# Attention over a cached K and V on one core: K loaded by transposing DMAs instead of transposed on TensorE

## The chip, the cores and the metric

The kernel runs on one core of a Trainium2 chip, in one launch. The metric is the time on the device in microseconds; smaller is better. The engines are TensorE (PE in the profile, PEld for its weight loads), VectorE (DVE), ScalarE (ACT), GpSimd (POOL) and SyncE (SP), which here only issues loads.

## The reference

Two independent attention blocks, A and B, of the same shapes are computed and their outputs put side by side. All inputs are bfloat16.

```python
B, Sq, D = 16, 64, 640
H, Sk, Dh = 32, 512, 128
q = (x @ wq).reshape(B, Sq, H, Dh).transpose(0, 2, 1, 3)
scores = einsum("bhqd,bhkd->bhqk", q, k_cache) * (Dh ** -0.5)
p = softmax(scores, axis=-1)
o = einsum("bhqk,bhkd->bhqd", p, v_cache)
out = o.transpose(0, 2, 1, 3).reshape(B, Sq, H * Dh) @ wo        # per block
result = concatenate([out_A, out_B], axis=-1)
```

For each batch entry and head there is a K and a V of 512 x 128 (128 KB each), used once, by 64 queries. K and V of both blocks together are 268 MB of the 295 MB that are read.

## The kernel before, in words

The unit of work is a step pair, called m, of two heads. One head is treated for two batch entries at a time (j = 0 and 1), so that the 64 queries of each fill the 128 partitions together. A group is one pair of batch entries with 16 of the 32 heads, eight m. A pass is one block and one half of the heads; there are 4 passes with 8 groups each, 256 m in all. The output of the first half of the heads is kept in `outp` and added to that of the second half (OVF), and the result is stored.

The operations for one m are:

- LDK and LDV (SyncE): loads of K and V for four heads and one batch entry, 512 KB each; a chunk, two m, has two of each. There are rings of 5 chunks for K and V.
- KX (TensorE, line 433): eight transposes of 128 x 128 for one batch entry into a PSUM bank, twice for each m; KE (VectorE, line 442): the copy of that bank into `ktp_ring`. After this d is on the partitions and the keys are along the row.
- QP2 (line 451): the queries, ten matmuls; QE2 (ScalarE, 459) evicts them.
- SM2 (467): the scores of two heads, four matmuls with 512 columns each; MX (VectorE, 476): the negative row maximum; EX (ScalarE, 482): the exponential with the row sum; RC2 (VectorE, 488): the reciprocal of the sums of two heads.
- NM (GpSimd, 496): the probabilities times the reciprocal. The write puts the keys in the order in which V has them on the partitions.
- TR2 (505): eight transposes of the probabilities; TE2 (VectorE, 512) evicts them; PV2 (524): sixteen matmuls with V; OE2 (ScalarE, 532); OP2 (540 and 545): the output projection, accumulated in PSUM over the 16 heads of a group.
- XT and XE (604, 612): the transposes of x for a later group, once in eight m; they use the same PSUM bank as TR2.

The order on each engine is written out by hand as templates, (kind, offset in m, sub):

```python
PE_T = (("TR2", 1), ("QP2", 4), ("KX", 4, 0), ("SM2", 3), ("PV2", 1), ("XT", 0), ("OP2", 0), ("KX", 4, 1))
DVE_T = (("TE2", 1), ("RC2", 2), ("KE", 4, 0), ("MX", 3, 0), ("MX", 3, 1), ("KE", 4, 1), ("OVF", 0))
```

In turn k, TensorE transposes the probabilities of m = k+1, projects the queries of k+4, makes the scores of k+3, and so on. `build_plan` expands the templates, puts the loads in an order by the times at which they are due and their slots come free, and finds from the tiles read and written which operation waits for which. Each PSUM tile (the transposes, the scores of each head, the queries, the output of attention) has one buffer. The program for each engine is then a plain list; SyncE's loads are all on one queue.

K is loaded with 8 keys on end in a partition's run of 2 KB, two heads on 128 partitions; V with 4 keys, 1 KB.

Of the kernel before, what the change touches and what calls it, by code (L numbers as in the profile page):

```python
# [5 lines left out]
BF16 = mybir.dt.bfloat16  # L6
# [8 lines left out]
class Cfg:  # L15
    G = 4
    HH = 16
    NKB = 5
    NVB = 5
    NX = 2  # L20
    NXN = 1
    XLEAD = 10
    NQ = 2
    NKT = 2
    NP = 4
    NPN = 3
    NT = 2
    NO = 2
    NR = 8
    PE_T = (("TR2", 1), ("QP2", 4), ("KX", 4, 0), ("SM2", 3), ("PV2", 1), ("XT", 0), ("OP2", 0), ("KX", 4, 1))  # L30
    ACT_T = (("QE2", 4), ("OE2", 1), ("XE", 0), ("EX", 3, 0), ("EX", 3, 1), ("OV", 0), ("ST", -1))
    DVE_T = (("TE2", 1), ("RC2", 2), ("KE", 4, 0), ("MX", 3, 0), ("MX", 3, 1), ("KE", 4, 1), ("OVF", 0))
    POOL_T = (("NM", 0, 0), ("NM", 0, 1))
    TAIL_SPLIT = 2
    SLOT_NS = 3600.0
# [3 lines left out]
class Op:  # L39
# [3 lines left out]
    def __init__(self, eng, kind, idx, reads=(), writes=(), dur=0.0, ts=None, aux=None):  # L43
# [12 lines left out]
        self.dma = kind in ("LDK", "LDV", "LDX", "LDWQ", "LDWO", "ST")  # L56


STAGES = ("LDW", "LDX", "LDK", "LDV", "KX0", "KE0", "KX1", "KE1", "QP2", "QE2", "SM2", "MX0", "MX1", "EX0", "EX1",
          "RC2", "NM0", "NM1", "TR2", "TE2", "XT", "XE", "PV2", "OE2", "OP2", "OV", "ST")  # L60
STAGE_IDX = {s: i for i, s in enumerate(STAGES)}
SUB_KINDS = ("KX", "KE", "EX", "NM", "MX")


def build_plan(dims, cfg):
    NBLK, B, H = dims["NBLK"], dims["B"], dims["H"]
    G = cfg.G
# [23 lines left out]
    def mk(eng, kind, idx, reads, writes, stage, m_ts, sub=0, aux=None, dur=0.0):  # L91
        return Op(eng, kind, idx, reads, writes, dur=dur, aux=aux, ts=(m_ts, STAGE_IDX[stage], sub))

    OFF = {}
    for t in cfg.PE_T:
        OFF.setdefault(t[0], t[1])

    def make_op(kind, m, sub):
        g0, g1 = 2 * m, 2 * m + 1
        ps_, bp, grp, h0 = step_info(g0)  # L100
        c = g0 // G
        if kind == "KX":
            return mk("pe", "KX", (m, sub), [("kn", c % cfg.NKB, g0 % G), ("kn", c % cfg.NKB, g1 % G), ("ident",)],
                      [("KTB",)], "KX%d" % sub, m, sub)
        if kind == "KE":
            return mk("dve", "KE", (m, sub), [], [("KTB",), ("ktp", m % cfg.NKT, sub)], "KE%d" % sub, m, sub)
        if kind in ("MX", "EX", "NM"):
            g = 2 * m + sub
            r = g % cfg.NR
# [18 lines left out]
        if kind == "QE2":  # L128
            return mk("act", "QE2", m, [], [("QB",), ("qT", m % cfg.NQ)], "QE2", m)
        if kind == "SM2":  # L130
            return mk("pe", "SM2", m, [("qT", m % cfg.NQ), ("ktp", m % cfg.NKT, 0), ("ktp", m % cfg.NKT, 1)],
                      [("SB", 0), ("SB", 1)], "SM2", m)
        if kind == "RC2":
            return mk("dve", "RC2", m, [("rowsum", r0), ("rowsum", r1)], [("recip", r0), ("recip", r1)], "RC2", m)
# [29 lines left out]

    templates = {"pe": cfg.PE_T, "dve": cfg.DVE_T, "pool": cfg.POOL_T, "act": cfg.ACT_T}
    for eng, tmpl in templates.items():
        offs = [t[1] for t in tmpl] + [cfg.XLEAD]
        for k in range(-max(offs), NMAC - min(offs)):
            for t in tmpl:
                kind, off = t[0], t[1]  # L170
                sub = t[2] if len(t) > 2 else 0
                if kind in ("XT", "XE"):
                    op = make_op(kind, k, 0)
# [3 lines left out]
                m = k + off  # L177
                if 0 <= m < NMAC:
                    op = make_op(kind, m, sub)
# [26 lines left out]
    for grp in range(NGRP):  # L206
        m0 = MPG * grp
        op = mk("sp", "LDX", grp, [], [("xn", grp % cfg.NXN)], "LDX", m0 - cfg.XLEAD + OFF["TR2"], aux=grp,
                dur=cfg.DMA_NS["LDX"])
# [10 lines left out]

    for c in range(NCHUNK):
        m0 = MPC * c
        for kind, ring, n_ring, cons, tb in (("LDK", "kn", cfg.NKB, "KX", 2), ("LDV", "v", cfg.NVB, "PV2", 2.5)):
            ready = NEG if c < n_ring else MPC * (c - n_ring + 1) - 1 - OFF[cons]
            for pi, (piece, j, hlo, hhi) in enumerate(chunk_pieces(c)):
                op = mk("sp", kind, (c, j, piece), [], [(ring, c % n_ring, gi) for gi in range(hlo, hhi)], kind,
                        m0, aux=(c, j, hlo, hhi, piece), dur=cfg.DMA_NS[kind] * (hhi - hlo) / 8.0)
                loads.append((ready, m0 - OFF[cons] + 0.01 * hlo, tb + 0.001 * pi, op))
    pending = sorted(loads, key=lambda e: (e[1], e[2]))
    t_now = min(e[1] for e in loads) - 4.0  # L230
    while pending:
        cand = [e for e in pending if e[0] <= t_now]
        if cand:
            e = cand[0]
        else:
            e = min(pending, key=lambda e_: (e_[0], e_[1], e_[2]))
# [110 lines left out]
def mha_kernel(nc, blocks, out, cfg=None):  # L347
    cfg = cfg or Cfg()
# [3 lines left out]
    _, H, SK, DH = k0.shape  # L352
    assert SQ == 64 and DH == 128 and SK == 512 and D % 128 == 0 and B % 2 == 0
    KT = D // 128
    G = cfg.G
    scale = float(DH) ** -0.5
    DN = D
    assert DN <= 1024
    N0 = min(DN, 512)
    N1 = DN - N0  # L360

# [1 line left out]
    prune_waits(progs)  # L363
    NBP, SPB, NHALF = info["NBP"], info["SPB"], info["NHALF"]
    HH = SPB
    NKB, NVB, NX, NXN, NQ, NKT, NP, NPN, NT, NO, NR = (cfg.NKB, cfg.NVB, cfg.NX, cfg.NXN, cfg.NQ, cfg.NKT, cfg.NP,
                                                       cfg.NPN, cfg.NT, cfg.NO, cfg.NR)

    def step_info(g):
        grp = g // SPB  # L370
# [7 lines left out]
    with contextlib.ExitStack() as es:  # L378
        block = es.enter_context(nc.Block())

        def sb(name, shape, dt):
            return es.enter_context(nc.sbuf_tensor(name, shape, dt))

        wq_sb = sb("wq_sb", [128, 2, KT, HH * DH], BF16)
        wo_sb = sb("wo_sb", [128, 2, HH, DN], BF16)
        outp = sb("outp", [128, NBP, DN], F32) if NHALF > 1 else None
        xT_ring = sb("xT_ring", [128, NX, KT, 128], BF16)
        xn_ring = sb("xn_ring", [128, NXN, D], BF16)
        kn_ring = sb("kn_ring", [128, NKB, 2, G // 2, 8, DH], BF16)
        v_ring = sb("v_ring", [128, NVB, 2, G, 4, DH], BF16)  # L390
        ktp_ring = sb("ktp_ring", [128, NKT, 2, 2, SK], BF16)
        qT_ring = sb("qT_ring", [128, NQ, 2, 128], BF16)
        p_ring = sb("p_ring", [128, NP, SK], BF16)
        pn_ring = sb("pn_ring", [128, NPN, SK], BF16)
# [7 lines left out]
        ident = sb("ident", [128, 128], BF16)  # L402
        ps = es.enter_context(nc.psum_tensor("ps", [128, 8, 512], F32))
# [9 lines left out]
        else:  # L413
            out_ps_all = ps[:, 0, 0:DN]
        S_BANK0 = 2
        PT_BANK, O_BANK, Q_BANK, KT_BANK = 4, 5, 6, 7
        pt_ps_flat = ps[:, PT_BANK, :].bitcast(BF16)
        pt_ps = pt_ps_flat.rearrange("p (s t q) -> p s t q", s=2, t=4)
        o_ps = ps[:, O_BANK, 0:256]
        q_ps = ps[:, Q_BANK, 0:256]  # L420
        kt_ps_flat = ps[:, KT_BANK, :].bitcast(BF16)
        kt_ps = kt_ps_flat.rearrange("p (t s) -> p t s", t=8)

        def s_bank(sub):
            return ps[:, S_BANK0 + sub, :]

        def em_KX(e, op):
            m, j = op.idx
            g0 = 2 * m
            c, hp = g0 // G, (g0 % G) // 2  # L430
            first = last = None
            for t8 in range(8):
                ins = e.transpose(kt_ps[:, t8, :], kn_ring[:, c % NKB, j, hp, t8, :], ident[:, :])  # L433
                first = first or ins
                last = ins
            return first, last

        def em_KE(e, op):
            m, j = op.idx
            src = kt_ps_flat.rearrange("p (t hs pp) -> p t hs pp", t=8, hs=2)  # L440
            dst = ktp_ring[:, m % NKT, :, j, :].rearrange("p hs (t pp) -> p t hs pp", t=8)
            ins = e.tensor_copy(dst, src)  # L442
            return ins, ins

        def em_QP2(e, op):
            m = op.idx
# [15 lines left out]
        def em_SM2(e, op):  # L462
            m = op.idx
            first = last = None
            for sub in range(2):
                for j in range(2):
                    ins = e.matmul(s_bank(sub)[64 * j:64 * j + 64, :], qT_ring[:, m % NQ, sub, 64 * j:64 * j + 64],  # L467
                                   ktp_ring[:, m % NKT, sub, j, :], start=True, stop=True, tile_position=(0, 64 * j))
                    first = first or ins
                    last = ins  # L470
            return first, last
# [19 lines left out]
        def em_NM(e, op):  # L491
            g = op.idx
            r = g % NR
            src = p_ring[:, g % NP, :].rearrange("q (th tl pp) -> q th tl pp", th=2, tl=4)
            dst = pn_ring[:, g % NPN, :].rearrange("q (tl pp th) -> q th tl pp", tl=4, th=2)
            ins = e.tensor_scalar(dst, src, recip[:, r:r + 1], 1.0, ALU.mult, ALU.mult)  # L496
            return ins, ins

# [117 lines left out]
        def em_LDKV(e, op):  # L616
            c, j, hlo, hhi, _piece = op.aux
            blk, bp, grp, ps_, hh0 = step_info(c * G)
            h0 = (ps_ % NHALF) * HH + hh0
            if op.kind == "LDV":  # L620
                src = blocks[blk][2][2 * bp + j, h0 + hlo:h0 + hhi].rearrange("g (p t) d -> p g t d", p=128)
                ins = e.dma_start(v_ring[:, c % NVB, j, hlo:hhi], src)
            else:
                src = blocks[blk][1][2 * bp + j, h0 + hlo:h0 + hhi].rearrange("(hp hs) (p t) d -> (hs p) hp t d",
                                                                              hs=2, t=8)
                ins = e.dma_start(kn_ring[:, c % NKB, j, hlo // 2:hhi // 2], src)  # L626
            return ins, ins

        emitters = dict(KX=em_KX, KE=em_KE, QP2=em_QP2, QE2=em_QE2, SM2=em_SM2, MX=em_MX, EX=em_EX, RC2=em_RC2,
                        NM=em_NM, TR2=em_TR2, TE2=em_TE2, PV2=em_PV2, OE2=em_OE2, OP2=em_OP2, OV=em_OV,  # L630
                        OVP=em_OVP, OVF=em_OVF, ST=em_ST, XT=em_XT, XE=em_XE, INIT1=em_INIT1, INIT2=em_INIT2,
                        LDWQ=em_LDWQ, LDWO=em_LDWO, LDX=em_LDX, LDK=em_LDKV, LDV=em_LDKV)
# [87 lines left out]
```

## Time and profile before

| what | value |
|---|---|
| time, median of 2 runs | 958.89 us (958.25 to 959.54) |
| span of the profiled execution (its own time) | 956.8 us |
| TensorE busy, matmuls | 919.4 us |
| VectorE busy | 841.9 us |
| ScalarE busy | 567.1 us |
| GpSimd busy | 416.9 us |
| mean granted TensorE clock | 0.998 |
| loads (queue q1) | 294.69 MB, 91.0% of 16 engines' time |

The span runs from the first to the last instruction of one profiled execution; the median of the timed runs lies 2.1 us above it. The profile page gives busy times for each engine, then the span cut into 40 slices of 23.9 us (busy tenths, granted clock, DMA share and GB/s), the DMA queues, the chain of work that ended last, and groups of like instructions with their busy time, mean duration, the idle time before them and what ended it.

### The profile page before, as it was taken

The numbers are of one execution on the slowest core, as the hardware profiler recorded it, in microseconds if no ns is written. First come the engines' busy times: TensorE is split into PE (matmuls) and PEld (weight loads), VectorE is DVE, ScalarE is ACT, GpSimd is POOL, SyncE is SP. The second block draws the span as 40 slices with busy tenths as digits, with TensorE's granted clock in tenths as the row PEclk, the third lists the DMA queues.
The fourth block names the chain that finished last, engine by engine and source line by source line (L and its number), as shares of the span: only waits on it lengthen the run. The fifth ranks groups of instructions, "written<-read, shape, count | busy, mean of one in ns | idle before, by whom it ended". The sixth has DMA issues, their size and how long they took to land.

```text
span 956.8 us, 34351 instructions
## 1 busy us (share of the span) xinstructions
PE 919.4 (96%) x14755; PEld 733.5 (77%) x15008; DVE 841.9 (88%) x1552; ACT 567.1 (59%) x1585; POOL 416.9 (44%) x518
## 2 busy tenths in 40 slices
PE   4999999999999999999999999999999999999997
PEld 3877777778777777877777787777877778777775
DVE  2898899898899999899999899889899998999996
ACT  1666656666665565656566666666666656565654
POOL 0444444444444444444444444444444444444443
PEclk9999999999999999999999999999999999999999
DMA  9999999999999999888999999988888988899830
GB/s 315 364 365 364 351 365 367 365 368 351 338 337 337 343 330 315 299 292 305 322 332 352 326 353 327 306 294 296 302 305 288 308 301 297 295 297 314 295 124 15
DMA packets 230871, 299.51 MB, mean 313 GB/s; under 512 B 9536, under 2 KB 165184, under 8 KB 230720
## 3 DMA queue, kind: packets, MB, share of 16 engines
q1 hardware_dynamic: 228416, 294.69, 91.0%
q8 instruction: 118, 1.93, 0.8%
q10 hardware_dynamic: 2304, 2.62, 0.8%
q14 instruction: 33, 0.27, 0.1%
HBM read 294.65 MB, written 2.62 MB: 311 GB/s over the span
## 4 chain that ended last, share of the span: by engine, by line
PE 89%; DVE 4%; POOL 3%; issue 2%; SPq 1%; DMA 1%; POOLq 0%; DVEq 0%
PE ps L433 22%; PE ps L524 14%; PE ps L451 14%; PE ps L467 14%; PE ps L505 12%; PE ps L545 7%; PE ps L540 5%; POOL pn_ring L496 3%; DVE out_sb L560 1%; DVE ktp_ring L442 1%; DVE pT_ring L512 1%; PE ps L604 1%; DMA xn_ring<-in_A_x_dram 1%; SPq L626 1%; SPq L583 1%
## 5 line engine op out<-in xcount | busy, mean ns | idle before, releaser
L496 POOL TENSOR_SCALAR pn_ring<-p_ring,recip 128x512 bf16<-128x512 bf16 x512 | 416.3, 843 | 532.7 <-DVE recip L488 532.7
L442 DVE COPY ktp_ring<-ps 128x1024 bf16<-128x1024 bf16 x512 | 353.7, 691 | 105.3 <-PE ps L433 85.1
L482 ACT ACTIVATE p_ring<-ps,negmax 128x512 bf16<-128x512 f32 x512 | 345.6, 684 | 4.8 <-DVE negmax L476 4.8
L476 DVE TENSOR_REDUCE negmax<-ps 128x1 f32<-128x512 f32 x512 | 327.3, 681 | 0.4 <-PE ps L467 0.3
L433 PE MATMUL ps<-ident,kn_ring 128*128 128x128 bf16 x4096 | 314.6, 220 | 2.8 <-DMA kn_ring<-in_A_k_cache_dram 1.6
L532 ACT ACTIVATE oT_ring<-ps 128x256 bf16<-128x256 f32 x256 | 98.0, 383 | 306.0 <-PE ps L524 306.0
L433 PEld LDWEIGHTS ps<-ident,kn_ring 128*128 128x128 bf16 x4096 | 251.9, 98 | 34.2 <-DVE ktp_ring L442 2.6
L524 PEld LDWEIGHTS ps<-pT_ring,v_ring 128*128 128x128 bf16 x4096 | 133.5, 98 | 109.2 <-issue 100.0
L451 PE MATMUL ps<-xT_ring,wq_sb 128*128 128x128 bf16 x2560 | 186.4, 220 | 3.2 <-DMA wq_sb<-in_A_wq_dram 3.2
L512 DVE COPY pT_ring<-ps 128x1024 bf16<-128x1024 bf16 x256 | 174.5, 682 | 4.6 <-PE ps L505 3.8
L524 PE MATMUL ps<-pT_ring,v_ring 128*128 128x64 bf16 x4096 | 163.8, 194 | 3.3 <-issue 1.7
L467 PE MATMUL ps<-ktp_ring,qT_ring 128*64 128x512 bf16 x1024 | 159.8, 392 | 0.4 <-ACT p_ring L482 0.4
L505 PE MATMUL ps<-ident,pn_ring 128*128 128x128 bf16 x2048 | 156.7, 219 | 3.5 <-POOL pn_ring L496 3.5
L451 PEld LDWEIGHTS ps<-xT_ring,wq_sb 128*128 128x128 bf16 x2560 | 155.2, 98 | 3.5 <-DMA wq_sb<-in_A_wq_dram 3.5
L459 ACT ACTIVATE qT_ring<-ps 128x256 bf16<-128x256 f32 x256 | 98.4, 384 | 66.8 <-PE ps L451 66.8
L505 PEld LDWEIGHTS ps<-ident,pn_ring 128*128 128x128 bf16 x2048 | 124.1, 98 | 7.0 <-POOL pn_ring L496 6.7
L545 PE MATMUL ps<-wo_sb,oT_ring 128*128 128x128 bf16 x512 | 112.1, 219 | 13.4
L482 ACT ACTIVATION_READ_ACCUMULATOR p_ring<-ps,negmax 128x1 f32 x512 | 105.0, 205 | 0.0
L540 PE MATMUL ps<-wo_sb,oT_ring 128*128 128x512 bf16 x259 | 97.8, 379 | 0.0
L540 PEld LDWEIGHTS ps<-wo_sb,oT_ring 128*128 128x128 bf16 x512 | 50.1, 98 | 30.6 <-ACT oT_ring L532 0.3
L467 PEld LDWEIGHTS ps<-ktp_ring,qT_ring 128*64 128x64 bf16 x1024 | 36.1, 108 | 27.1 <-ACT p_ring L482 0.6
L545 PEld LDWEIGHTS ps<-wo_sb,oT_ring 128*128 128x128 bf16 x512 | 50.1, 98 | 0.0
(13 smaller groups left out, 112.7 us busy)
## 6 DMA issues: line engine op xcount, KB each, us to landing
kn_ring<-in_A_k_cache_dram SPq DMA_DIRECT2D x128, 512.0 KB, 7.0
v_ring<-in_A_v_cache_dram SPq DMA_DIRECT2D x128, 512.0 KB, 7.2
kn_ring<-in_B_k_cache_dram SPq DMA_DIRECT2D x126, 512.0 KB, 4.8
v_ring<-in_B_v_cache_dram SPq DMA_DIRECT2D x126, 512.0 KB, 5.7
wq_sb<-in_A_wq_dram SPq DMA_DIRECT2D x8, 640.0 KB, 10.4
wo_sb<-in_A_wo_dram SPq DMA_DIRECT2D x8, 640.0 KB, 10.2
wq_sb<-in_B_wq_dram SPq DMA_DIRECT2D x8, 640.0 KB, 8.4
wo_sb<-in_B_wo_dram SPq DMA_DIRECT2D x8, 640.0 KB, 7.5
```

The source lines that it names most:

```text
L433: ins = e.transpose(kt_ps[:, t8, :], kn_ring[:, c % NKB, j, hp, t8, :], ident[:, :])
L442: ins = e.tensor_copy(dst, src)
L451: ins = e.matmul(q_ps[:, sub * 128:(sub + 1) * 128], wq_sb[:, ps_ % 2, kt, hh * DH:(hh + 1) * DH], xT_ring[:, grp % NX, kt, :], start=(kt ...
L467: ins = e.matmul(s_bank(sub)[64 * j:64 * j + 64, :], qT_ring[:, m % NQ, sub, 64 * j:64 * j + 64], ktp_ring[:, m % NKT, sub, j, :], start=T ...
L476: ins = e.reduce_max(negmax[:, r:r + 1], s_bank(g % 2), axis=AX.X, negate=True)
L482: ins = e.activation(p_ring[:, g % NP, :], s_bank(g % 2), ACTF.Exp, bias=negmax[:, r:r + 1], scale=1.0, accum_out=rowsum[:, r:r + 1])
L496: ins = e.tensor_scalar(dst, src, recip[:, r:r + 1], 1.0, ALU.mult, ALU.mult)
L505: ins = e.transpose(pt_ps[:, sub, t, :], pn_ring[:, g % NPN, t * 128:(t + 1) * 128], ident[:, :])
L512: ins = e.tensor_copy(pT_ring[:, m % NT].rearrange("p s t q -> p (s t q)"), pt_ps_flat)
L524: ins = e.matmul(o_ps[:, col:col + 64], v_ring[:, c % NVB, j, gi, t, :], pT_ring[:, m % NT, sub, t, 64 * j:64 * j + 64], start=(t == 0), s ...
L540: ins = e.matmul(out_ps0, oT_ring[:, m % NO, sub, :], wo_sb[:, ps_ % 2, hh, 0:N0], start=(hh == 0), stop=(hh == SPB - 1))
L545: last = e.matmul(out_ps1, oT_ring[:, m % NO, sub, :], wo_sb[:, ps_ % 2, hh, N0:DN], start=(hh == 0), stop=(hh == SPB - 1))
```

## The change

K is no longer loaded as it lies in memory and then transposed. Each K load becomes a transposing DMA on the same queue, which puts d on the partitions itself. Its source is seen as rows of 32 keys x 128 d (8 KB), 16 rows to a head and 64 to a load of four heads. In `kt_ring` a partition holds, for each of the 32 places in a row, the 64 rows' values; a head's keys are so 32 runs of 16 elements at a step of 64. KX, KE, their places in the templates, `ktp_ring` and the PSUM bank go away. SM2 reads `kt_ring`, and waits for the load. The order of the keys in the scores is another one, (place in the row, row), so NM reads and writes with new patterns to arrive at the order that V has, which does not change. The ready time of a K load follows from SM2 (offset 3) instead of KX (offset 4).

```diff
-    NKT = 2
+    KR = 16
-    PE_T = (("TR2", 1), ("QP2", 4), ("KX", 4, 0), ("SM2", 3), ("PV2", 1), ("XT", 0), ("OP2", 0), ("KX", 4, 1))
+    PE_T = (("TR2", 1), ("QP2", 4), ("SM2", 3), ("PV2", 1), ("XT", 0), ("OP2", 0))
-    DVE_T = (("TE2", 1), ("RC2", 2), ("KE", 4, 0), ("MX", 3, 0), ("MX", 3, 1), ("KE", 4, 1), ("OVF", 0))
+    DVE_T = (("TE2", 1), ("RC2", 2), ("MX", 3, 0), ("MX", 3, 1), ("OVF", 0))
...
-            return mk("pe", "SM2", m, [("qT", m % cfg.NQ), ("ktp", m % cfg.NKT, 0), ("ktp", m % cfg.NKT, 1)],
+            return mk("pe", "SM2", m, [("qT", m % cfg.NQ), ("kn", c % cfg.NKB, g0 % G), ("kn", c % cfg.NKB, g1 % G)],
...
-        for kind, ring, n_ring, cons, tb in (("LDK", "kn", cfg.NKB, "KX", 2), ("LDV", "v", cfg.NVB, "PV2", 2.5)):
+        for kind, ring, n_ring, cons, tb in (("LDK", "kn", cfg.NKB, "SM2", 2), ("LDV", "v", cfg.NVB, "PV2", 2.5)):
...
+    KR, KJ = cfg.KR, SK // cfg.KR
...
-        kn_ring = sb("kn_ring", [128, NKB, 2, G // 2, 8, DH], BF16)
+        kt_ring = sb("kt_ring", [128, NKB, 2, KJ, G * KR], BF16)
-        ktp_ring = sb("ktp_ring", [128, NKT, 2, 2, SK], BF16)
...
-                                   ktp_ring[:, m % NKT, sub, j, :], start=True, stop=True, tile_position=(0, 64 * j))
+                                   kt_ring[:, c % NKB, j, :, gi * KR:(gi + 1) * KR], start=True, stop=True, tile_position=(0, 64 * j))
...
-            src = p_ring[:, g % NP, :].rearrange("q (th tl pp) -> q th tl pp", th=2, tl=4)
-            dst = pn_ring[:, g % NPN, :].rearrange("q (tl pp th) -> q th tl pp", tl=4, th=2)
+            src = p_ring[:, g % NP, :].rearrange("q (jj t r) -> q t jj r", jj=8, t=4)
+            dst = pn_ring[:, g % NPN, :].rearrange("q (t r jj) -> q t jj r", t=4, jj=8)
...
-                src = blocks[blk][1][2 * bp + j, h0 + hlo:h0 + hhi].rearrange("(hp hs) (p t) d -> (hs p) hp t d",
-                                                                              hs=2, t=8)
-                ins = e.dma_start(kn_ring[:, c % NKB, j, hlo // 2:hhi // 2], src)
+                src = blocks[blk][1][2 * bp + j, h0 + hlo:h0 + hhi].rearrange("g (r t) d -> (g r) (t d)", t=KJ)
+                ins = e.dma_start_transpose(kt_ring[:, c % NKB, j, :, hlo * KR:hhi * KR], src)
```

## The prediction

> **What bounds the kernel now.** I read the engine totals first, then the chain that ended last, then the groups of the two lines that go away, then the DMA parts, and at the end the last 20 us of the timeline, where the work to be removed has already run out.
>
> ```profile
> span 956.8 us, 34351 instructions
> PE 919.4 (96%) x14755; PEld 733.5 (77%) x15008; DVE 841.9 (88%) x1552; ACT 567.1 (59%) x1585; POOL 416.9 (44%) x518
> ...
> GB/s 315 364 365 364 351 365 367 365 368 351 338 337 337 343 330 315 299 292 305 322 332 352 326 353 327 306 294 296 302 305 288 308 301 297 295 297 314 295 124 15
> ...
> q1 hardware_dynamic: 228416, 294.69, 91.0%
> q8 instruction: 118, 1.93, 0.8%
> ...
> PE 89%; DVE 4%; POOL 3%; issue 2%; SPq 1%; DMA 1%; POOLq 0%; DVEq 0%
> ...
> L496 POOL TENSOR_SCALAR pn_ring<-p_ring,recip 128x512 bf16<-128x512 bf16 x512 | 416.3, 843 | 532.7 <-DVE recip L488 532.7
> L442 DVE COPY ktp_ring<-ps 128x1024 bf16<-128x1024 bf16 x512 | 353.7, 691 | 105.3 <-PE ps L433 85.1
> ...
> L433 PE MATMUL ps<-ident,kn_ring 128*128 128x128 bf16 x4096 | 314.6, 220 | 2.8 <-DMA kn_ring<-in_A_k_cache_dram 1.6
> ```
>
> TensorE carries 89% of the chain, and line 433, the K transposes, is the largest single line in it (22%). But the second resource is close. Queue q1, all the loads, keeps the sixteen DMA engines 91% busy. The GB/s row shows two regimes: until about slice 10 the loads run flat against 365 to 368 GB/s while they fill the rings; later they fall to some 300 because SyncE waits for TensorE to free K slots. I take 366 GB/s as the ceiling of plain loads. Moving 294.69 MB at it takes 805 us: only 152 us under the span. Whatever TensorE gives up beyond that is not to be had unless the DMA gets cheaper too, and this change makes the DMA do more.
>
> The third limit is a ring of dependences. In the last steps no K transposes are left, and the timeline shows what remains between one group of probability transposes (line 505) and the next:
>
> ```profile
> 947.16 0.62 PE L505 MATMUL ps<-ident,pn_ring 128*128 128x128 bf16 x8 [0.56 <-POOL pn_ring L496]
> ...
> 947.82 0.69 DVE L512 COPY pT_ring<-ps 128x1024 bf16<-128x1024 bf16 x1 [1.00 <-PE ps L505]
> 948.43 0.16 DVE L488 RECIPROCAL recip<-rowsum 128x2 f32<-128x2 f32 x1
> ...
> 948.68 1.61 POOL L496 TENSOR_SCALAR pn_ring<-p_ring,recip 128x512 bf16<-128x512 bf16 x2 [1.57 <-DVE recip L488]
> ...
> 950.34 0.62 PE L505 MATMUL ps<-ident,pn_ring 128*128 128x128 bf16 x8 [0.56 <-POOL pn_ring L496]
> ```
>
> TR2, its eviction TE2, the reciprocal RC2 queued behind it on VectorE, two NM on GpSimd, and the next TR2: 950.34 - 947.16 = 3.18 us per step of two heads. The whole run averages (950.34 - 24.52) / 255 = 3.63 us, the first TR2 being at 24.52. So the ring is the floor of the compute side once TensorE is relieved, at 3.18 us.
>
> **The change part by part.** TensorE loses 4096 transposes. Eight of them hold the issue for about 0.45 us (in the timeline the weight loads of line 433 start at 601.40 and those of line 505 behind them at 601.85), two groups a step, so about 0.9 to 1.05 us of 3.57 in a steady step; TensorE alone would then need 2.5 us a step, under the ring. VectorE loses 512 copies of 691 ns, 1.38 us a step; what stays is 842 - 354 = 488 us, and VectorE bounds nothing. The stall moves to the ring or to the DMA.
>
> Compute side, if data is always there: 24.5 to the first TR2, 255 x 3.18 = 811, plus 32 steps with x transposes (one showed 605.71 - 601.85 = 3.86 against 3.57, so 0.29 each, 9 us), plus 6.5 from the last TR2 to the end: 851 us.
>
> DMA side. V, weights and x, 294.69 - 134.22 = 160.47 MB, stay as they are: 438 us at 366 GB/s. K is 16 x 32 x 512 x 128 elements in each of two blocks, 134.22 MB, in 256 loads' worth of 512 KB. A transposing DMA is not in the trace. From below: no better than plain loads, 1.43 us per 512 KB or 367 us in all; a gain under that is excluded by the flat 366, which holds for mixed rows of 1 and 2 KB, so 8 KB source rows have no dip to repair. From above: the slowest row of bytes per engine time is the instruction queue q8, 1.93 MB in 0.8% of the span, 7.65 us, 252 GB/s; at that K costs 2.08 us a load, 532 us in all. The destination speaks for the slow end: each partition used to receive runs of 2 KB and now gets 32 runs of 64 elements, 128 bytes. A transfer that scatters into short runs is nearer to the slow row than to the plain one, so I take 252 GB/s. Sum: 2 until data flows + 532 + 438 + 12 from the last score matmuls to the end (944.87 to 956.8) = 984 to 985, and the median of the runs lies 2.1 above the profiled span: 987 us. The DMA side is then 134 us above the compute side, and the ring's 3.18 us is hidden.
>
> The skill is of two minds here. "Advanced Engine Details and Errata", section "X-Bar Transpose (TRN2)", says that transposing DMAs run about as fast as plain ones, 350 to 400 GB/s; "DMA: Bandwidth & Descriptors", section "Latency and other measured facts", gives 261 GB/s as measured where the middle dimension isn't contiguous, and asks for reads of at least 4 KB, which rows of 8 KB meet. By 350 GB/s K would take an estimated 383 us and the compute side would decide; by 261 GB/s an estimated 514 us, and the end would come at about 969. No run here shows either yet.
>
> Smaller edits. SM2 (line 467) waits for the DMA's K slot instead of KE, and reads K in runs of 16 elements: four matmuls of 392 ns; I cost the strided read at nothing, since TensorE would have 3.8 - 2.5 = 1.3 us spare in a step; without that cover it costs what it adds, and above 0.3 us a matmul it would decide. Behind a late SM2 on TensorE are PV2 and OP2, and VectorE's MX waits for it, so a late K stalls all. SyncE issues as many loads as before, in nearly the same order, K slots freed one step later (10 steps of buffer); four issues a chunk of two steps take about 1.9 us now (0.88 at 602.10, 0.99 at 605.33) against 7.6 us, so even doubled they are covered. V, x and weights queue behind K on that same queue.
>
> NM (line 496) changes its order: it read 256 elements on end and wrote at a step of 4 bytes; it now reads 16 on end and writes at a step of 16 bytes. From below 843 ns, since the element count is equal and a gain has no source; from above GpSimd's other tensor operation, the identity's affine select, 293 ns for 128 elements, 2.29 ns each, 1.17 us for 512. I take 843, the same operation on the same data; being in the ring twice, each 0.1 us more costs 0.2 us a step, hidden up to a ring of 3.70 us, that is an NM of 1.10 us.
>
> **The rivals.**
>
> Rival 1, the other side: transposing costs no more than copying. Then the DMA side is 2 + 367 + 438 + 12 = 819, the ring decides with 851, and the time is 853 with the 2.1. For it: long source rows and the same bytes. Against: the 128-byte runs. It holds as long as K's rate stays above 366 x 367 / 399 = 336 GB/s; at 289 GB/s (464 us for K) the gain has shrunk to 4%, at 268 (500 us) to nothing.
>
> Rival 2: transposes and copies don't overlap. Now a 512 KB load lands 4.8 to 7.0 us after issue though its data takes 1.43, so several are in flight and hide each other's latency. The last V loads of 256 KB, with little else in flight, land after 3.1 us of which 0.7 is data: 2.4 us of latency to be exposed. If each transposing DMA exposes a fifth of that, 0.5 us, 256 of them add 128 us: 1115. It decides from the first exposed 0.1 us, since the DMA side is already the longer one. Against it: the semaphores order only consumers, and nothing in the program drains the queue.
>
> Rival 3: NM becomes the bound. At 1.17 us the ring is 3.18 + 0.65 = 3.83, and 24.5 + 255 x 3.83 + 9 + 6.5 + 2 = 1019. For it: the write step is four times wider. Against: it is at the far end of its bounds. The skill's "GPSIMD Engine Reference", section "Performance pitfalls for Q7 kernels", charges half as much again for reads stepping over more than 8 bytes and is silent on writes; applied to the write it would give an estimated 1.26 us and a time near 1065. No run here shows it.
>
> Rival 4: TensorE's clock falls when it starves. After the gap of 4.71 us before 23.27 the eight transposes at 24.53 took 1.03 us instead of 0.62, while steady gaps are under 1 us at a granted 0.998. My forecast leaves gaps of about 1.3 us a step, so I price it at nothing and give it no chance of its own.
>
> **How the numbers follow.** The forecast, DMA-bound with K near 250 to 290 GB/s, 940 to 1040: 0.42. Rival 1, up to 940: 0.30. Rival 2, above 1040: 0.18. Rival 3: 0.10. A measurement of this kernel tells about 2% from no change, 939.7 to 978.1. Faster by more has rival 1 and a little of the forecast's lower edge, 0.32; within 2%, 0.18 from the lower half of the forecast; slower, its upper half and rivals 2 and 3, 0.50. The forecast's own range is 940 to 1040. The range that should hold 8 times in 10 reaches from the ring's floor, 850, to the fifth of latency exposed, 1115.
>
> **What would show it right or wrong.** Right: the DMA row at 9 in all slices to the end, GB/s lower than now at about 300, TensorE idle before SM2 released by the K load, VectorE near 490 us busy, NM at 843 ns. Rival 1: about 345 GB/s and the timeline's period of line 505's successor at 3.2 us with the waits on NM. Rival 2: GB/s below 270 with engines under 9 tenths busy, or SyncE held at its transposing issues. Rival 3: NM above 1.1 us and TR2 waiting for it all along. My price for K is the weakest term: it hangs on one row of another kind of transfer.

## The result, and the profile after

The changed kernel takes 1768.87 us (1767.24 to 1770.49, 2 runs) against 958.89: a ratio of 1.845, 95% interval 1.840 to 1.850. The forecast was 987 with a range of 850 to 1115. It was slower, as forecast, but by 810 us instead of 28, and for a reason that the prediction had put among its rivals, with its price far too small.

The page of the changed kernel, the parts that answer to those shown of the kernel before:

```profile
span 1765.4 us, 25784 instructions
...
PE 1098.4 (62%) x10784; PEld 729.4 (41%) x10912; DVE 537.7 (30%) x1040; ACT 570.1 (32%) x1585; POOL 1235.2 (70%) x518
...
PEclk9977777777777777757777777777777777777776
...
q1 hardware_dynamic: 691296, 294.70, 65.1%
...
POOL 70%; PE 15%; DVE 11%; issue 3%; SPq 1%; DMA 0%; POOLq 0%; ACT 0%; DVEq 0%
...
L473 POOL TENSOR_SCALAR pn_ring<-p_ring,recip 128x512 bf16<-128x512 bf16 x512 | 1234.5, 2603 | 521.3 <-DVE recip L465 521.3
L482 PE MATMUL ps<-ident,pn_ring 128*128 128x128 bf16 x2048 | 252.5, 300 | 629.1 <-POOL pn_ring L473 628.3
```

GpSimd, no part of the bound before (3% of the chain), now carries 70% of it. NM went from 843 ns to 2603 ns with the same number of elements. The DMA row is at 0% of the chain and q1 at 65%: the transposing loads are not what the end waits for. The granted clock of TensorE is down to seven tenths, 0.758 in the mean. VectorE is down to 538 us, not to the 488 forecast: in the kernel before, the busy times of its three largest lines (354, 327 and 175 us) already add up to more than its 842, so they overlap, and the engine gains less than the line takes away.

One turn of the ring in the timeline, from TR2 to TR2:

```profile
904.16 1.03 PE L482 MATMUL ps<-ident,pn_ring 128*128 128x128 bf16 x8 [2.61 <-POOL pn_ring L473]
...
905.23 0.69 DVE L489 COPY pT_ring<-ps 128x1024 bf16<-128x1024 bf16 x1 [2.73 <-PE ps L482]
905.84 0.16 DVE L465 RECIPROCAL recip<-rowsum 128x2 f32<-128x2 f32 x1
906.09 4.82 POOL L473 TENSOR_SCALAR pn_ring<-p_ring,recip 128x512 bf16<-128x512 bf16 x2 [1.98 <-DVE recip L465]
...
910.97 1.03 PE L482 MATMUL ps<-ident,pn_ring 128*128 128x128 bf16 x8 [2.60 <-POOL pn_ring L473]
```

The period is 910.97 - 904.16 = 6.81 us; it was 3.18 at the tail of the kernel before. Two terms account for it: the pair of NM takes 4.82 instead of 1.62 (3.20 more) and TR2 1.03 instead of 0.62 (0.41 more). 255 turns of 6.81 are 1737 of the 1765 us.

Three questions stay: is NM's order alone enough for it, what would the transposing DMA cost if NM were cheap, and what is the clock's part?

### The profile page after: what moved, and what is told of

It is laid out like the page before. It is cut to its first block, busy times and chain, and to the rows that moved or that the text cites. A ratio compares the mean times of both kernels' runs of the same rounds, so it can differ in the third digit from the quotient of the medians.

```text
span 1765.4 us, 25784 instructions
## 1 busy us (share of the span) xinstructions
PE 1098.4 (62%) x10784; PEld 729.4 (41%) x10912; DVE 537.7 (30%) x1040; ACT 570.1 (32%) x1585; POOL 1235.2 (70%) x518
## 3 DMA queue, kind: packets, MB, share of 16 engines
q8 instruction: 86, 1.41, 0.3%
## 4 chain that ended last, share of the span: by engine, by line
POOL 70%; PE 15%; DVE 11%; issue 3%; SPq 1%; DMA 0%; POOLq 0%; ACT 0%; DVEq 0%
POOL pn_ring L473 70%; PE ps L482 14%; DVE pT_ring L489 10%; SPq L602 1%; DVE recip L465 1%; DMA xn_ring<-in_A_x_dram 0%; POOLq L374 0%; SPq L560 0%; PE ps L517 0%; SPq L599 0%; PE ps L501 0%; DVE out_sb L537 0%; PE ps L581 0%; ACT xT_ring L589 0%; PE ps L522 0%
## 5 line engine op out<-in xcount | busy, mean ns | idle before, releaser
L473 POOL TENSOR_SCALAR pn_ring<-p_ring,recip 128x512 bf16<-128x512 bf16 x512 | 1234.5, 2603 | 521.3 <-DVE recip L465 521.3
L482 PE MATMUL ps<-ident,pn_ring 128*128 128x128 bf16 x2048 | 252.5, 300 | 629.1 <-POOL pn_ring L473 628.3
L482 PEld LDWEIGHTS ps<-ident,pn_ring 128*128 128x128 bf16 x2048 | 187.8, 135 | 719.9 <-POOL pn_ring L473 642.9
L426 PE MATMUL ps<-xT_ring,wq_sb 128*128 128x128 bf16 x2560 | 315.0, 306 | 5.0 <-DMA wq_sb<-in_A_wq_dram 4.5
L426 PEld LDWEIGHTS ps<-xT_ring,wq_sb 128*128 128x128 bf16 x2560 | 273.4, 146 | 6.4 <-issue 3.3
L444 PE MATMUL ps<-kt_ring,qT_ring 128*64 128x512 bf16 x1024 | 265.7, 620 | 1.6 <-DMA kt_ring<-in_A_k_cache_dram 1.6
L501 PE MATMUL ps<-pT_ring,v_ring 128*128 128x64 bf16 x4096 | 194.8, 208 | 1.7 <-issue 1.7
L517 PE MATMUL ps<-wo_sb,oT_ring 128*128 128x512 bf16 x384 | 143.1, 409 | 0.0
L444 PEld LDWEIGHTS ps<-kt_ring,qT_ring 128*64 128x64 bf16 x1024 | 46.1, 138 | 50.4 <-issue 46.7
L465 DVE RECIPROCAL recip<-rowsum 128x2 f32<-128x2 f32 x256 | 39.6, 155 | 0.9 <-ACT p_ring L459 0.9
```

Of the source, the lines that this page charges most:

```text
L426: ins = e.matmul(q_ps[:, sub * 128:(sub + 1) * 128], wq_sb[:, ps_ % 2, kt, hh * DH:(hh + 1) * DH], xT_ring[:, grp % NX, kt, :], start=(kt ...
L482: ins = e.transpose(pt_ps[:, sub, t, :], pn_ring[:, g % NPN, t * 128:(t + 1) * 128], ident[:, :])
L501: ins = e.matmul(o_ps[:, col:col + 64], v_ring[:, c % NVB, j, gi, t, :], pT_ring[:, m % NT, sub, t, 64 * j:64 * j + 64], start=(t == 0), s ...
L517: ins = e.matmul(out_ps0, oT_ring[:, m % NO, sub, :], wo_sb[:, ps_ % 2, hh, 0:N0], start=(hh == 0), stop=(hh == SPB - 1))
```

## The experiments

**The prices by themselves.** A kernel that loads in stages and then runs NM with eight orders, with nothing else on the chip but the store of the output, which overlaps the first order:

```diff
+            for i in range(NB):                       # NB = 24; also with kr = 32 and 128
+                transp(sync, NB + i, i, 16).then_inc(sems[1], 16)
+            sync.wait_ge(sems[1], 16 * NB)
...
+                nm(p[:, :].rearrange("q (jj t r) -> q t jj r", jj=8, t=4),
+                   pn[:, :].rearrange("q (t r jj) -> q t jj r", t=4, jj=8))
```

> Measures the disputed prices by themselves and computes nothing of the reference: stages of 24 loads of 512 KB each (K plain in 2 KB runs; K transposing from rows of 8, 4 and 1 KB; two transposing and two V loads in turn; V plain in 1 KB runs), each stage waited for, then eight NM each with eight orders of reading and writing, with no DMA running. Theory 1 (only NM was mis-priced): a write at a step of 16 bytes costs 2.6 us on a quiet chip, a plain one at most 0.85, and 24 transposing loads from 8 KB rows take 24 x 2.08 = 50 us against 34 for plain ones. Theory 2 (the transposing DMA was mis-priced too): they take 24 x 2.8 = 67 us, which is what the share of engine time in the changed kernel's queue comes to (1149 us of 16 engines, less 438 for the other loads, 711 for K). Theory 3 (the DMA's short writes slow GpSimd): NM with a write step of 16 bytes costs about 0.85 us here. On the orders: if the write step decides, 4 bytes cost 0.84, 8 bytes lie between, and reading at a step of 128 bytes with a plain write is cheap; if the read runs of 16 decide, runs of 16 on both sides cost 2.6.

The groups of NM in windows of the timeline, smallest, median and largest duration in ns; the orders follow each other as listed in the table below (a window can hold one instruction of its neighbour):

```profile
L96 POOL TENSOR_SCALAR pn<-p,rc x7: 691/691/692, 313.3 to 318.0; 128x512 bf16<-128x512 bf16 x7
L96 POOL TENSOR_SCALAR pn<-p,rc x8: 691/831/832, 318.8 to 325.1; 128x512 bf16<-128x512 bf16 x8
L96 POOL TENSOR_SCALAR pn<-p,rc x8: 831/831/832, 326.0 to 332.5; 128x512 bf16<-128x512 bf16 x8
L96 POOL TENSOR_SCALAR pn<-p,rc x5: 1395/1396/1396, 334.4 to 340.3; 128x512 bf16<-128x512 bf16 x5
L96 POOL TENSOR_SCALAR pn<-p,rc x9: 1396/2527/2528, 344.8 to 364.6; 128x512 bf16<-128x512 bf16 x9
L96 POOL TENSOR_SCALAR pn<-p,rc x8: 691/691/1121, 368.0 to 373.5; 128x512 bf16<-128x512 bf16 x8
L96 POOL TENSOR_SCALAR pn<-p,rc x6: 1120/1120/1120, 374.7 to 380.8; 128x512 bf16<-128x512 bf16 x6
L96 POOL TENSOR_SCALAR pn<-p,rc x7: 2526/2527/2527, 385.8 to 401.6; 128x512 bf16<-128x512 bf16 x7
```

| read | write | ns |
|---|---|---|
| on end | on end (step 2 B) | 691 |
| on end | step 4 B (the order of the kernel before) | 831 |
| runs of 64 | step 4 B | 831 |
| runs of 32 | step 8 B | 1396 |
| runs of 16 | step 16 B (the change) | 2527 |
| runs of 16 | runs of 16 | 691 |
| step 128 B | on end | 1120 |
| on end | step 16 B | 2527 |

The write's step decides: at 16 bytes NM takes 2527 ns whether it reads in runs of 16 or on end. From 4 bytes on the duration lies on a line: 8 B is 565 ns above 4 B, 16 B another 1131, so 141 ns for each byte of step. The short read runs cost nothing (691 with runs of 16 on both sides), and even a read at a step of 128 bytes costs less than half of the write at 16. The DMA moved at most 1 GB/s while the 16-byte writes ran, so theory 3, that the DMA's writes slow GpSimd, falls.

The DMA in windows of the same run (columns: window in us, its length, GpSimd's busy time with its count, clock, DMA share, GB/s); 40 to 90 lies in the stage of 8 KB rows, 100 to 160 mostly in that of 4 KB, 161 to 220 in that of 1 KB, with the pause before it:

```profile
1.00:31.00 30.00, 8.86 (x3) 1.00 1.00 369
...
40.00:90.00 50.00, 0.00 (x0) 1.00 1.01 205
...
100.00:160.00 60.00, 0.00 (x0) 1.00 1.06 203
161.00:220.00 59.00, 0.00 (x0) 1.00 1.13 209
```

and the rate in slices of a quarter of a microsecond, from 50 to 60 us:

```profile
GB/s 52 140 290 289 290 293 288 85 40 130 139 153 269 291 289 293 288 192 50 188 159 11 89 257 269 290 290 292 202 39 42 168 152 182 270 286 290 293 284 276
```

A transposing load costs 524,288 B / 205 GB/s = 2.56 us where a plain one takes 1.43, and the length of the source rows changes little. The slices show how: the data flow at some 290 GB/s for about 1.25 us, then for 1.25 to 1.5 us the rate lies between 11 and 202, once in each 2.5 to 2.75 us, which is one load. At 290 throughout a load would take 1.81 us, so these holes cost some 0.75 us of each. Plain loads in the same run have none: from 10 to 20 us, in slices of the same length, they lie between 369 and 401. So theory 2 was nearer than theory 1, if not as far as its 2.8 us.

**NM alone, on the kernel before.**

```diff
-            src = p_ring[:, g % NP, :].rearrange("q (th tl pp) -> q th tl pp", th=2, tl=4)
-            dst = pn_ring[:, g % NPN, :].rearrange("q (tl pp th) -> q th tl pp", tl=4, th=2)
+            src = p_ring[:, g % NP, :].rearrange("q (jj t r) -> q t jj r", jj=8, t=4)
+            dst = pn_ring[:, g % NPN, :].rearrange("q (t r jj) -> q t jj r", t=4, jj=8)
```

> The kernel before with only the changed kernel's reading and writing order in NM (the keys then don't meet those of V; that part is left wrong). Theory 1: NM 2.6 us, the ring 6.8 us a step, 24.5 + 255 x 6.8 + 7 = 1766 us. Theory 3: NM close to 0.85 us and the time close to 959.

1691.62 us. NM alone makes 733 of the 810 us, with K loaded and transposed as before. The expectation took TR2 cold, as in the changed kernel; here TensorE has the K transposes as well (its mean clock is 0.898), and TR2 takes 0.62 us in most turns, 1.03 in some:

```profile
897.61 4.83 POOL L496 TENSOR_SCALAR pn_ring<-p_ring,recip 128x512 bf16<-128x512 bf16 x2 [1.94 <-DVE recip L488]
...
902.49 0.62 PE L505 MATMUL ps<-ident,pn_ring 128*128 128x128 bf16 x8 [1.44 <-POOL pn_ring L496]
904.00 4.83 POOL L496 TENSOR_SCALAR pn_ring<-p_ring,recip 128x512 bf16<-128x512 bf16 x2 [1.57 <-DVE recip L488]
```

904.00 - 897.61 = 6.39 us, 0.01 above 3.18 + 3.20.

A middle point, the kernel before with a write step of 8 bytes (`jj=4` in both lines):

> The kernel before with NM writing at a step of 8 bytes (read in runs of 32; the keys then don't meet those of V, that part is left wrong): NM 1.40 us on the quiet chip. Theory: the ring of 3.18 us grows by 2 x (1.40 - 0.83) to 4.32 and passes TensorE's 3.57: 24.5 + 255 x 4.32 + 9 + 6.5 + 2 = 1144 us. Rival (GpSimd has slack, 44% busy, and hides it): 959.

1117.65 us, with NM at 1414 ns in the profile. GpSimd's idle 56% did not hide it; NM was in a ring that TensorE's 3.57 us covered by only 0.4 us. The 26 us less than expected fit the overlap of a pair of NM: the pair at 604.32 us takes 2.66 instead of twice 1.41, and the turn 4.21 (TR2 at 602.82 and 607.03) instead of 4.32. The 16-byte pairs show it too (4.82 us for two of 2.60).

**The change without the transposing DMA.** K is loaded by plain DMAs into the same places, so TensorE and VectorE are relieved all the same. In this and the other kernels with plain K the last chunk is also loaded whole instead of in two pieces:

```diff
-                ins = e.dma_start_transpose(kt_ring[:, c % NKB, j, :, hlo * KR:hhi * KR], src)
+                dst = kt_ring[:, c % NKB, j].rearrange("p t r -> p (t r)").rearrange("p (hp t d) -> p hp t d", hp=2, t=8)
+                ins = e.dma_start(dst[:, hlo // 2:hhi // 2], src)        # src as in the kernel before
```

> The changed kernel with K loaded by plain DMAs in the same places (what SM2 reads is then not K with d on the partitions; that part is left wrong) and NM as in the change, its write stepping 16 bytes. Theory (NM alone sets the 1769 us, the transposing DMA none of it): 1740 to 1775 us. Rival (the transposing DMA carries part of it): below 1650.

1767.77 us, where the change has 1768.87: beside this NM, the transposing loads cost nothing that shows.

> As the kernel with plain K loads, and NM with the reading and writing order of the kernel before (0.84 us): the change as it would be if neither price had been paid. Theory (the sum of the prediction's compute side): the ring of 3.18 us decides, 853 us. Rival (another ring or the DMA decides): 880 or more.

861.31 us, 8 over the expected 853; the turn in its timeline is 3.19 us (TR2 at 601.98 and 605.17). Its page shows the ring on the path, POOL first, TensorE and VectorE next:

```profile
POOL 35%; PE 22%; DVE 20%; SPq 6%; ACT 6%; DMA 6%; issue 4%; POOLq 0%; DVEq 0%
...
L473 POOL TENSOR_SCALAR pn_ring<-p_ring,recip 128x512 bf16<-128x512 bf16 x512 | 415.0, 839 | 436.6 <-DVE recip L465 436.6
L482 PE MATMUL ps<-ident,pn_ring 128*128 128x128 bf16 x2048 | 159.2, 221 | 77.3 <-POOL pn_ring L473 68.9
```

> As the kernel with plain K loads, and NM reading and writing on end (0.69 us). Theory: the ring falls by 2 x 0.15 to 2.88, 24.5 + 255 x 2.88 + 9 + 6.5 + 2 = 777 us, under the DMA side of 819 + 2, which now decides: 821 us. Rival (still bound by dependences): 850.

845.45 us, against 821 expected: a miss, though a small one. The chain now names ScalarE (31%), TensorE (25%) and the DMA (17%), so neither the ring through NM nor the DMA alone decides. SM2's weight load waits 82.9 us for EX, which frees the score banks, a ring for which the sum had no term; that this ring makes the 24 us is not shown.

**The transposing DMA with a cheap NM.** The changed kernel with NM on end (the line is `src = p_ring[:, g % NP, :]`, `dst` alike):

> The changed kernel with NM reading and writing on end: the keys of the probabilities then don't meet those of V, which is the part left wrong. Theory 1: NM falls to 0.84 us or less, the ring of TR2, TE2, RC2 and NM to 3.2 us, and the DMA decides: 987 us, K at 252 GB/s. Theory 2: K at some 190 GB/s, 2 + 711 + 438 + 12 = 1163 us. Theory 3: NM stays above 1.5 us and the time above 1200.

1250.01 us. Its page, with the waits no longer at GpSimd:

```profile
span 1248.2 us, 25912 instructions
...
GB/s 229 267 241 244 249 242 259 242 224 232 252 256 249 234 248 224 254 234 245 241 240 252 242 219 246 246 247 225 235 237 226 245 243 249 228 243 249 219 238 187
...
SPq 42%; DMA 30%; PE 18%; ACT 8%; issue 2%; POOL 0%; DVE 0%; POOLq 0%; ACTq 0%; DVEq 0%
```

The loads bound it: some 240 GB/s to the end. But the largest part of the chain is SyncE, and 36% is its line 602, the issuing of the transposing loads. One issue holds SyncE for a median of 3.9 to 4.2 us, against 2.4 in the staged run and 0.4 to 0.7 for a plain K load in the kernel before; SyncE also waits 253 us for K slots. The V loads stand behind on the same queue, and it is for V that TensorE waits: 274 us before PV2, against 41 for K before SM2.

And with `KR = 128`, source rows of 1 KB, for which V's order needs no permutation at all and the whole reference is computed:

> The changed kernel with source rows of 1 KB (4 keys) instead of 8 KB: the keys then come out in V's order and NM reads and writes on end; the whole reference is computed. Theory 1: if the length of the source rows doesn't matter to the DMA, the same time as with NM plain and 8 KB rows, about 987; if short rows cost the DMA, longer than that. Theory 2: 1163 or more.

1248.02 us. Row length is again of no matter, and the NM of the change was avoidable without any cost to the DMA; but even so the kernel is 30% slower than before. In both, if the other loads cost their 438 us, K costs (1248 - 14 - 438) / 256 = 3.11 us a load, 0.55 more than alone.

**Does the sum of the loads hold when the DMA decides?** Plain loads, each K load followed by another of the same size that nothing reads:

> As the kernel with plain K loads and NM on end, with each K load followed by a second one of as many bytes that nothing reads (and rings of 3 chunks for K): K then costs the DMA 2 x 1.43 = 2.87 us for each 512 KB that is used, more than the transposing loads' 2.56 alone. Theory (in a DMA-bound run the sum over the loads holds, and what the transposing kernels take above it, 1248 against 1109, comes of transposing): 2 + 734 + 438 + 12 + 2 = 1188 us. Rival (being DMA-bound costs a tenth by itself, in late waits): 1300 or more.

1186.09 us, 2 from the expected 1188, with the rate flat at about 372 GB/s. So with plain loads, being bound by the DMA does not itself cost anything over the sum, and the 140 us that the transposing kernels take above 1109 (2 + 655 + 438 + 12 + 2, with K at 2.56 us a load) come with transposing. The mixing of the two kinds is, by the staged run, the smaller part of it. The staged run has a stage with two transposing loads and two of V in turn, in which none waits for a slot, and behind it one with V alone:

```profile
230.00:269.00 39.00, 0.00 (x0) 1.00 1.00 252
269.00:304.00 35.00, 0.00 (x0) 1.00 1.03 320
```

At 252 GB/s one load of each kind takes 4.16 us. With V at 1.43 us that leaves 2.73 for the transposing one, with V at the 1.64 of the stage behind it 2.52: of the 0.55 us at most 0.17 shows here. Whether the rest comes of SyncE, held by its issues and by the K slots with V behind, or of the DMA engines, no run shows; nor does one show a kernel with only some of K transposed by DMA, which would have to balance TensorE against the DMA.

**The clock.** As the kernel with plain K and the 16-byte NM, with idle work for TensorE behind each OP2:

```diff
+            for i in range(32):
+                last = e.transpose(ps[:, 7, :].bitcast(BF16)[:, 0:128], ident[:, :], ident[:, :])
```

> As the kernel with plain K loads and NM's write stepping 16 bytes (1768 us; what SM2 reads is not K with d on the partitions), with 32 idle transposes of the identity into an unused PSUM bank behind each OP2, which nothing waits for. Theory W (the clock that falls while TensorE waits for NM lengthens the ring by TR2's 1.03 instead of 0.62 us): TR2 goes back to some 0.62, the granted clock rises from 0.745, and the time falls by 255 x 0.41 = 105 us to about 1665, less so if the clock is not fully regained. Rival (the ring is GpSimd's alone): 1768, or more by the added work.

1674.49 us: 93 us faster by added work.

```profile
PEclk9999999999999999999999999999999999999999
...
L473 POOL TENSOR_SCALAR pn_ring<-p_ring,recip 128x512 bf16<-128x512 bf16 x512 | 1239.4, 2616 | 421.9 <-DVE recip L465 421.9
L482 PE MATMUL ps<-ident,pn_ring 128*128 128x128 bf16 x2048 | 159.2, 221 | 445.4 <-POOL pn_ring L473 444.7
```

NM is the same, TR2's matmuls are back at 221 ns from 305, the clock is at 9 tenths or more throughout.

## Why the prediction was wrong

The account, all from runs: relieving TensorE and VectorE is worth 958.89 - 861.31 = 98 us. NM's write step costs 1674.49 - 861.31 = 813 us (the ring says 255 x 3.20 = 816). TensorE's lower clock costs 93. The transposing DMA costs 1, being hidden, and 1250.01 - 845.45 = 405 where nothing hides it. The first terms, 813 + 93 + 1 - 98, give the 810 us (but for rounding) by construction, as differences of runs that follow on one another; the independent check is the ring's 816.

- The compute side, 853 us, was right to 1% (861), and with it the 3.18 us read from the tail, where the work to be removed had run out. The ring was the right thing to look at.
- The step that failed is NM's term, taken at 843 ns with an upper bound of 1.17 us, and with it the statement that the ring's 3.18 us is hidden: NM took 2603 ns and the ring 6.81 us. The bound came from the identity's affine select, another operation of that engine, which reads and writes on end. It bounds nothing about steps, and the trace of before holds one write step only, 4 bytes. The mechanism was rival 3's, at 0.10 and 1019 us. The prediction saw that a tenth of a microsecond of NM costs 0.2 a step, and that the cover was used up at 1.10, and still let a row of another access order close the range. The Trainium skill's 50% from "GPSIMD Engine Reference", section "Performance pitfalls for Q7 kernels", is for reads; the runs here give 62% for a read at 128 bytes (1120 against 691), and 266% for a write at 16.
- K's price was too low: 2.08 us assumed, 2.56 measured alone, 3.11 in the kernel. The slow row taken as an upper end was not one either. That K costs more than a plain load was right, but the reason given, runs of 128 bytes at the destination, is not borne out: with source rows of 1 KB a partition's runs are 1 KB, and the rate is 209 GB/s instead of 205. Rival 2, transposes and copies that don't overlap, names the size that was measured (0.5 us a load assumed, 0.55 in the kernel), but the staged mixture shows at most 0.17 of it, so the match is in part luck; its sign, SyncE held at its transposing issues, was there. With NM cheap the time is 1250, also outside the range. The forecast's own edges did not follow from its sum either: K at 290 GB/s gives 917 us and not 940, and 1040 needs 229 GB/s. Neither rate of the Trainium skill was reached in the mean: "Advanced Engine Details and Errata", section "X-Bar Transpose (TRN2)", has 350 to 400 GB/s, "DMA: Bandwidth & Descriptors" 261 in its section "Latency and other measured facts"; measured here are 205 in the mean and 290 while it flows.
- Rival 4, the clock, was priced at nothing for the forecast's gaps of 1.3 us. For a kernel that waits for loads this was right: the kernel with doubled plain loads had a mean clock of 0.886 and still met its sum within 2 us. But a lengthened ring opens the gaps, and TR2 is in the ring, so rival 3 brings rival 4 with it; the prediction priced them apart.
- SM2's strided reading of K, costed at nothing, costs nothing: 394 ns a matmul in the kernel with plain K and NM as before, against 392. SyncE's issues were mis-sized. The prediction had them covered even if doubled; a transposing one took a median of 2.3 to 2.4 us in the change against 0.4 to 0.7 for a plain one. Beside the slow NM that is 1% of the chain, with NM cheap 36%.

## What to carry to other kernels

When a change forces another order of elements on an operation, price the order, not only the count: a row of the same engine with a plain pattern is no upper bound, and a short run of that one instruction with the new pattern settles it. An engine that is idle for half of the time can still be in the ring that sets the pace; find the ring where the bound work is absent, such as the tail, and ask how much each member may grow before the cover is gone. And where a DMA takes over work near a balance of TensorE and DMA, compare the rate at which the total becomes equal (268 GB/s here) with a measured one before all else.

## What the runs showed of the hardware

- GpSimd's `tensor_scalar` on 512 bfloat16 elements a partition: 691 ns written on end, then 141 ns for each byte of write step from 4 bytes on, up to 2527 at 16. Runs of 16 elements on both sides cost no more than on end (691); reading at a step of 128 bytes costs 1120.
- A transposing DMA of 512 KB takes about 2.56 us whether its source rows are 8, 4 or 1 KB (205, 203 and 209 GB/s), in a rhythm of some 1.25 us at 290 GB/s and 1.25 to 1.5 us at 11 to 202. Its issue holds SyncE for a median of 2.4 us.
- Waits of 2.6 us before TR2, in turns of 6.8 us, went with a mean granted clock of 0.745 to 0.758, at which eight transposes took 1.03 us instead of 0.62; with waits of 1.8 us and idle work it stayed at 0.998. In the kernel before with the 16-byte NM, after waits of 2.65 and 2.66 us TR2 took 0.62 us at 122.24 and 1.03 at 135.12, with a mean clock of 0.898. So the length of one wait does not decide by itself; whether the share of idle time does, these runs don't separate. "TensorE: Matmul & The Clock Gate" of the Trainium skill, section "Why this matters for your kernels", warns of gaps above about 3 us; in the change no wait before TR2 was above 2.6 us between 100 and 380 us, and the mean clock there was 0.75.
